# Streamed weights of a recurrent attention and mixer kernel: single blocks instead of pairs, and the mixer's transfers issued from GpSimd

## The chip, the cores and the metric

One core of one Trainium2 chip. The metric is device time of the whole program in microseconds (us); lower is better. A verdict of "faster" or "slower" needs 2%.

## The reference

Four layers one after another on x of 2048 tokens by 640: a recurrent attention with memory (A), a token-shift mixer (B), then A and B again with the same weights. Cut to what matters:

```python
def _A_ref(x, mem0, Wq, Wk, Wv, Wo, seg_len):      # 32 heads of 192, segments of 32 tokens
    mem = mem0                                       # 8 memory tokens
    for s in range(n_seg):                           # 64 segments, strictly in turn
        h = concatenate([mem, x[:, s*32:(s+1)*32]])
        q, k, v = h @ Wq, h @ Wk, h @ Wv             # weights 640 x 6144 each
        o = softmax(mask(q k^T * scale)) v @ Wo      # weights 6144 x 640
        mem = o[:, :8]                               # the next segment needs it
        outs.append(o[:, 8:])

def _B_ref(x, w1, w2, w3, w4):
    h = gelu(layernorm(x) @ w1)                      # 640 x 640
    x1 = x + shift(h) @ w2                           # 640 x 640
    return x1 + gelu(layernorm(x1) @ w3) @ w4        # 640 x 1536, 1536 x 640
```

## The kernel before

Both A layers run at once, the second five segments behind the first, so that a step's weights serve two segments ("lanes"): 64 + 5 = 69 steps, of which the first five and the last five have one lane. The mixer works on chunks of two steps beside the attention (35 chunks). The weights do not fit on chip. Part of them stays, the rest is streamed in every step through a ring of slots that both users share. A plan in Python, with a model of each engine, fixes every engine's instruction order; the chip then follows that order with semaphores.

```python
RING = 8          # slots of two blocks (2 x 768 columns, bf16) for 128 partitions
RING_A = 7        # at most so many for attention's weights
RING_B = 3        # at most so many for the mixer's
DMA_SKEW = 1.6    # the plan's model of a landing
FLIGHT = 5        # SyncE's transfers in flight: number n waits for number n - 5
...
    def block(t, kind, g, c, due):            # attention's weights, 128 rows of Wq, Wk, Wv or Wo
        ...
        a = cut + (c - cut) // 2 * 2          # pairs of blocks
        if (t, kind, g, a) not in streamed:
            b = ring("ra")

            def fn(op):
                return nc.sync.dma_start(out=T(b)[:, 0:2 * n].rearrange("p (c n) -> p c n", c=2), in_=w_src(kind, g, a, a + 2))
            add("SP", 0.45, due, fn, w=(b,), dma=P * 2 * n * 2, queue="wa")
...
    def load_b(c, nm, n, due):                # the mixer's weights, pairs too
        ...
            def fn(op):
                return nc.sync.dma_start(out=T(b)[:, 0:(e - a) * Dm].rearrange("p (c n) -> p c n", n=Dm), in_=src)
            add("SP", 0.45, due, fn, r=rd, w=(b,), dma=P * (e - a) * Dm * 2, queue="wb")
...
    for o in placed:                          # the count of transfers in flight
        ins = o.fn(o)
        if o.dma and o.e == "SP":
            if len(flight) >= FLIGHT:
                tc.add_manual_dep(ins.ins, flight[-FLIGHT].ins.name, ...)
            flight.append(ins)
```

## Time and profile before

| | before |
|---|---|
| median of 4 runs | 3588.28 us (3584.36 to 3591.39) |
| TensorE (PE) busy | 95% of the span |
| the core's DMA engines busy | 94% |
| streamed transfers | 2277 of attention, 630 of the mixer |

How to read the views: PE is TensorE, DVE VectorE, ACT ScalarE, POOL GpSimd, SP SyncE; L536 is line 536 of the kernel, and `a <- b` says that a waited for b. psk, psq and psv are the products with Wk, Wq and Wv, psy that with Wo; psh, hs and y are the mixer's. wst is a slot of the ring, oT the attention's output that psy reads. wbd is a copy of w1, w3 and a part of w2 that the kernel lays out anew in device memory at its start.

The three stages (five steps of one lane, 59 of two, five of one) have to be read apart. Time of PE that is not work I sort by cause as follows, here and after: the distance between the starts of two consecutive matmuls, less the median distance of that shape, goes to what the trace says ended the wait; "fetch" is a wait that no semaphore ended. The sum of the medians is called PE's floor. The prediction shows the views and says what is in them.

### The profile page before, as it was taken

How to read it: one execution, taken by the hardware profiler on the slowest of the kernel's cores; microseconds unless marked ns; L12 is line 12 of the kernel's file. 1: busy time of each engine (PE TensorE's matmuls, PEld its weight loads, DVE VectorE, ACT ScalarE, POOL GpSimd, SP SyncE). 2: the span in 40 equal slices, each digit the busy share in tenths (PEclk: the TensorE clock that was granted, in tenths of full speed). 3: DMA queues.
4: the chain of work that ended last, by engine and by line, in shares of the span. 5: the costliest groups of instructions: out<-in, count | busy, mean ns of one | idle time of the engine just before them, and what ended most of it. 6: DMA issues, size and time to landing. Idle time of an engine off the chain costs nothing.

```text
span 3584.0 us, 188496 instructions
## 1 busy us (share of the span) xinstructions
PE 3387.8 (95%) x84703; PEld 3256.1 (91%) x84703; DVE 2375.3 (66%) x7085; ACT 1709.2 (48%) x3584; POOL 306.2 (9%) x522
## 2 busy tenths in 40 slices
PE   5889999999999999999999999999999999999996
PEld 4778999999999999999999999999999999999875
DVE  2456767767667666776666777776667667776555
ACT  2344545545455544455445554554545445544432
POOL 2000000000000000000000000000000000000000
PEclk9999999999999999999999999999999999999998
DMA  9999999999999999999999999999999999999996
GB/s 341 314 308 306 309 298 309 306 302 315 307 310 323 310 299 304 303 301 312 303 305 310 303 299 303 313 312 300 310 318 309 302 304 306 308 309 310 321 310 212
DMA packets 804793, 1097.18 MB, mean 306 GB/s; under 512 B 51982, under 2 KB 800540, under 8 KB 803984
## 3 DMA queue, kind: packets, MB, share of 16 engines
q1 hardware_dynamic: 795472, 1069.06, 91.2%
q0 software_dynamic: 8512, 16.08, 1.4%
q8 instruction: 662, 10.85, 1.2%
q14 instruction: 147, 1.20, 0.1%
HBM read 1079.68 MB, written 8.19 MB: 304 GB/s over the span
## 4 chain that ended last, share of the span: by engine, by line
PE 86%; DMA 8%; issue 4%; DVE 0%; ACT 0%; POOL 0%; SPq 0%; POOLq 0%; DVEq 0%; ACTq 0%
PE psy L675 16%; PE psk L536 15%; PE psv L577 15%; PE psq L536 15%; PE psvt L589 5%; PE pso L656 4%; PE pss L608 4%; PE psh L999 3%; DMA wst<-in_B_w_dram 3%; PE y L1017 3%; PE pst L641 2%; DMA wst<-in_A_Wk_dram 2%; PE hs L967 1%; DMA wst<-in_A_Wv_dram 1%; PE psh L945 1%
## 5 line engine op out<-in xcount | busy, mean ns | idle before, releaser
L536 PEld LDWEIGHTS <-wst 128*128 128x128 bf16 x13248 | 561.5, 100 | 36.0 <-issue 19.3
L662 DVE CAST oT<-pso 128x480 bf16<-128x480 f32 (+1 forms) x552 | 341.7, 619 | 379.7 <-PE pso L656 377.3
L593 ACT COPY V<-psvt 80x768 bf16<-80x768 bf16 (+1 forms) x552 | 438.4, 794 | 309.0 <-PE psvt L589 302.2
L675 PE MATMUL psy<-oT,wo 128*128 128x80 bf16 (+1 forms) x10350 | 491.6, 199 | 15.3 <-issue 8.6
L577 PE MATMUL psv<-hT,wv 128*128 128x80 bf16 (+1 forms) x9936 | 480.5, 199 | 12.3 <-issue 10.7
L544 ACT CAST qT<-psq 128x480 bf16<-128x480 f32 (+1 forms) x552 | 292.1, 529 | 400.5 <-PE psq L536 398.9
L536 PE MATMUL psq<-hT,wq 128*128 128x80 bf16 (+1 forms) x9936 | 454.2, 199 | 19.6 <-issue 10.0
L583 ACT CAST vTs<-psv 128x480 bf16<-128x480 f32 (+1 forms) x552 | 291.2, 528 | 362.7 <-PE psv L577 359.5
L536 PE MATMUL psk<-hT,wk 128*128 128x80 bf16 (+1 forms) x9936 | 452.8, 199 | 11.7 <-issue 9.3
L619 DVE CUSTOM_DVE_ANT_1 pss<-pss,mask 80x320 f32<-80x320 f32 (+1 forms) x512 | 246.0, 481 | 294.3 <-PE pss L608 287.8
L577 PEld LDWEIGHTS <-wv 128*128 128x128 bf16 x9936 | 408.4, 99 | 30.0 <-issue 11.0
L675 PEld LDWEIGHTS <-wo 128*128 128x128 bf16 x10350 | 413.3, 99 | 23.4 <-issue 15.3
L536 PEld LDWEIGHTS <-wq 128*128 128x128 bf16 x9936 | 395.2, 100 | 31.2 <-issue 13.3
L536 PEld LDWEIGHTS <-wk 128*128 128x128 bf16 x9936 | 397.9, 100 | 25.4 <-issue 14.3
L536 PE MATMUL psk<-hT,wst 128*128 128x80 bf16 (+1 forms) x6624 | 367.9, 199 | 12.1 <-issue 6.5
L577 PE MATMUL psv<-hT,wst 128*128 128x80 bf16 (+1 forms) x6624 | 353.2, 199 | 12.4 <-issue 8.2
L675 PE MATMUL psy<-oT,wst 128*128 128x80 bf16 (+1 forms) x6210 | 335.4, 199 | 11.2 <-issue 10.4
L536 PE MATMUL psq<-hT,wst 128*128 128x80 bf16 (+1 forms) x6624 | 331.6, 199 | 12.4 <-issue 9.4
L626 ACT ACTIVATE pss<-pss,sm 80x320 f32<-80x320 f32 (+1 forms) x552 | 262.0, 475 | 151.5 <-DVE sm L619 151.5
L631 DVE TENSOR_REDUCE sm<-pss 80x4 f32<-80x320 f32 (+1 forms) x552 | 252.3, 457 | 116.4 <-ACT pss L626 115.7
L552 DVE CAST kT<-psk 128x320 bf16<-128x320 f32 (+1 forms) x552 | 254.0, 460 | 112.7 <-PE psk L536 109.3
L646 ACT COPY PT<-pst 80x320 bf16<-80x320 bf16 (+1 forms) x552 | 221.9, 402 | 220.2 <-PE pst L641 218.1
(117 smaller groups left out, 5256.9 us busy)
## 6 DMA issues: line engine op xcount, KB each, us to landing
wst<-in_A_Wk_dram SPq DMA_DIRECT2D x552, 384.0 KB, 5.2
wst<-in_A_Wq_dram SPq DMA_DIRECT2D x552, 384.0 KB, 5.2
wst<-in_A_Wv_dram SPq DMA_DIRECT2D x552, 384.0 KB, 5.2
wst<-in_A_Wo_dram SPq DMA_DIRECT2D x621, 320.0 KB, 5.0
wst<-wbd SPq DMA_DIRECT2D x280, 320.0 KB, 5.1
wst<-in_B_w_dram SPq DMA_DIRECT2D x280, 320.0 KB, 5.7
wst<-wbd SPq DMA_DIRECT2D x70, 160.0 KB, 4.4
wk<-in_A_Wk_dram SPq DMA_DIRECT2D x8, 576.0 KB, 6.8
```

Of the source, the lines that this page charges most:

```text
L536: nc.tensor.matmul(out=o[:, c, 0:N], lhsT=w[:, c * P:(c + 1) * P], rhs=h[:, kc, c0:c0 + N], start=pq.begin(), stop=True, skip_group_check= ...
L544: nc.scalar.copy(out=q[:, :, 0:N], in_=T(pq)[:, :, 0:N])
L552: nc.vector.tensor_copy(out=k4[:, :, 0::3, 0:N], in_=p4[:, :, 0::2, 0:N])
L577: nc.tensor.matmul(out=o[:, c, 0:N], lhsT=w[:, c * P:(c + 1) * P], rhs=h[:, kc, c0:c0 + N], start=pv.begin(), stop=True, skip_group_check= ...
L583: nc.scalar.copy(out=vs[:, :, 0:N], in_=T(pv)[:, :, 0:N])
L593: nc.scalar.copy(out=V_[0:N, :, 0:Dh], in_=T(pt)[0:N].rearrange("n c f -> n (c f)").rearrange("n (i e) -> n i e", i=HG))
L619: nc.vector.tensor_tensor_reduce(out=o, in0=o, in1=maskt.unsqueeze(1).to_broadcast([N, HG, N]), scale=-scale, scalar=3.0e38, op0=ALU.add, ...
L626: nc.scalar.activation(out=o, in_=o, func=ACT.Exp, bias=sm_[0:N, 0:1], scale=-1.0)
L631: nc.vector.reduce_sum(out=sm_[0:N, 4:4 + HG], in_=o, axis=AX.X)
L646: nc.scalar.copy(out=Pt[0:N, :, 0:N], in_=T(pst)[0:N, :, 0:N])
L662: nc.vector.tensor_copy(out=o_[:, :, 0:N], in_=T(pso)[:, :, 0:N])
L675: nc.tensor.matmul(out=T(psy[j])[:, m - m0, c0:c0 + N], lhsT=w[:, m * P:(m + 1) * P], rhs=o_[:, c, 0:N], start=psy[j].begin(), stop=True, ...
```

## The change

The intent: a smaller grain lets a slot be reused as soon as one block is read, and lets a matmul begin as soon as its one block has landed. The doubled number of transfers is shared between two issuing engines. The bytes of the ring and of SyncE's transfers in flight stay.

```diff
-RING = 8
-RING_A = 7
-RING_B = 3
+RING = 16
+RING_A = 14
+RING_B = 6
+B_SP = False
+POOL_US = 0.9
+SP_US = 0.47
-DMA_SKEW = 1.6
-FLIGHT = 5
+DMA_SKEW = 2.0
+FLIGHT = 10
 ...
-        b.make = lambda: wring.tile([P, 2 * GW], bf16, name="wst", tag=f"r{b.slot}")
+        b.make = lambda: wring.tile([P, GW], bf16, name="wst", tag=f"r{b.slot}")
 ...
-                return nc.sync.dma_start(out=T(b)[:, 0:2 * n].rearrange("p (c n) -> p c n", c=2), in_=w_src(kind, g, a, a + 2))
-            add("SP", 0.45, due, fn, w=(b,), dma=P * 2 * n * 2, queue="wa")
+                return nc.sync.dma_start(out=T(b)[:, 0:n], in_=w_src(kind, g, c, c + 1)[:, 0, :])
+            add("SP", SP_US, due, fn, w=(b,), dma=P * n * 2, queue="wa")
 ...
+        def fn(op):
+            return (nc.sync if B_SP else nc.gpsimd).dma_start(out=T(b)[:, 0:Dm], in_=src)
+        add("SP" if B_SP else "POOL", SP_US if B_SP else POOL_US, due, fn, r=rd, w=(b,), dma=P * Dm * 2, queue="wb")
```

The count of transfers in flight looks at SyncE's alone, so the mixer's are no longer in it.

More of the change, by code (lines that the diff above doesn't have):

```diff
@@ L435, in fn @@
                     return nc.sync.dma_start(out=tl[:], in_=w_src(kind, g, 0, cut))
-                add("SP", 0.45, due, fn, w=(b,), dma=P * cut * n * 2, queue="wa")
+                add("SP", SP_US, due, fn, w=(b,), dma=P * cut * n * 2, queue="wa")
                 resident[kind, g] = b, tl
@@ L439, in block @@
             return b, lambda: tl[:, c, :]
-        a = cut + (c - cut) // 2 * 2
-        if (t, kind, g, a) not in streamed:
+        if (t, kind, g, c) not in streamed:
             b = ring("ra")
             def fn(op):
-                return nc.sync.dma_start(out=T(b)[:, 0:2 * n].rearrange("p (c n) -> p c n", c=2), in_=w_src(kind, g, a, a + 2))
-            add("SP", 0.45, due, fn, w=(b,), dma=P * 2 * n * 2, queue="wa")
-            streamed[t, kind, g, a] = b
-        b = streamed[t, kind, g, a]
@@ L449, in block @@
-        return b, lambda: T(b)[:, (c - a) * n:(c - a + 1) * n]
-    mixer = {}
-    def load_b(c, nm, n, due):
-        a = n - n % 2
-        e = min(a + 2, KC if nm in ("w1", "w2") else FC)
-        if (c, nm, a) not in mixer:
-            b = ring("rb")
-            k = {"w1": a, "w3": KC + a, "w2": KC + FC - 4 + a}.get(nm)
-            if nm == "w4":
-                src, rd = w4_v[:, a:e, :], []
-            elif nm == "w2" and a < 4:
-                src, rd = B_w2.rearrange("(g r) d -> r g d", r=QD)[0:P, a:e, :], []
-            else:
-                src = wbd[k:k + e - a].rearrange("b p n -> p b n")
-                rd = [B("wbd", k + i) for i in range(e - a)]
-            def fn(op):
-                return nc.sync.dma_start(out=T(b)[:, 0:(e - a) * Dm].rearrange("p (c n) -> p c n", n=Dm), in_=src)
-            add("SP", 0.45, due, fn, r=rd, w=(b,), dma=P * (e - a) * Dm * 2, queue="wb")
-            mixer[c, nm, a] = b
-        b = mixer[c, nm, a]
-        return b, lambda: T(b)[:, (n - a) * Dm:(n - a + 1) * Dm]
+                return nc.sync.dma_start(out=T(b)[:, 0:n], in_=w_src(kind, g, c, c + 1)[:, 0, :])
@@ new lines, in block @@
+            add("SP", SP_US, due, fn, w=(b,), dma=P * n * 2, queue="wa")
+            streamed[t, kind, g, c] = b
+        b = streamed[t, kind, g, c]
+        return b, lambda: T(b)[:, 0:n]
+    def load_b(c, nm, n, due):
+        b = ring("rb")
+        k = {"w1": n, "w3": KC + n, "w2": KC + FC - 4 + n}.get(nm)
+        if nm == "w4":
+            src, rd = w4_v[:, n, :], []
+        elif nm == "w2" and n < 4:
+            src, rd = B_w2[QD * n:QD * n + P, :], []
+        else:
+            src, rd = wbd[k], [B("wbd", k)]
+        def fn(op):
+            return (nc.sync if B_SP else nc.gpsimd).dma_start(out=T(b)[:, 0:Dm], in_=src)
+        add("SP" if B_SP else "POOL", SP_US if B_SP else POOL_US, due, fn, r=rd, w=(b,), dma=P * Dm * 2, queue="wb")
+        return b, lambda: T(b)[:, 0:Dm]
```

## The prediction

> **What bounds the kernel now.** I read the page first (busy shares, DMA queues), then three windows cut at the places where the work changes, then PE's waits inside the longest window, then a two-microsecond timeline of one such wait, and last the waits of the DMA-issuing queue.
>
> The page, busy shares and DMA queues:
>
> ```profile
> PE 3387.8 (95%) x84703; PEld 3256.1 (91%) x84703; DVE 2375.3 (66%) x7085; ACT 1709.2 (48%) x3584; POOL 306.2 (9%) x522
> ...
> q1 hardware_dynamic: 795472, 1069.06, 91.2%
> q0 software_dynamic: 8512, 16.08, 1.4%
> q8 instruction: 662, 10.85, 1.2%
> ```
>
> Two things are nearly full: TensorE (95%) and the DMA engines (91.2 + 1.4 + 1.2 = 94% with queue 14). Which of them sets the end has to be read by stage. The program runs 69 recurrent steps; in the first five and the last five only one of the two layers is at work, between them both. Cut there (a step begins where psk's 240 matmuls of it begin):
>
> ```profile
> 0.00:298.80 298.80, 232.67 (x6020) 202.25 (x6021) 124.24 (x479) 99.65 (x248) 35.05 (x65) 0.98 0.97 320
> 298.80:3288.90 2990.10, 2907.95 (x72341) 2838.04 (x72339) 2088.53 (x6034) 1497.83 (x3063) 246.00 (x412) 1.00 0.94 307
> 3288.90:3584.00 295.10, 247.21 (x6351) 215.77 (x6347) 162.51 (x574) 111.69 (x273) 25.10 (x45) 0.90 0.87 284
> ```
>
> First column after the window is its length, then PE's busy time; the last two are the DMA share and GB/s. In the first 299 us DMA is at 97% and PE has holes: that stage is bound by bytes (weights that stay are loaded too). The middle 2990 us, 83% of the time, is PE's: 2908 of 2990 us. I took every start-to-start distance of consecutive matmuls from the trace and put the median of its own shape in place of each: 36 ns for 128x80, 25 for 128x40, 56 for 128x128, 136 for 128x320. That sum, PE's floor in its present order, is 3246 us in all and 2868 us in the middle stage. So the middle stage loses only 122 us, 1.77 us a step of 50.7. PE's waits there tell to whom:
>
> ```profile
> PE psy L675 <- issue: 15.5, 25, 1.4
> PE psq L536 <- issue: 13.1, 21, 2.6
> PE psv L577 <- issue: 13.1, 19, 2.2
> PE y L1017 <- DMA wst<-in_B_w_dram: 10.8, 13, 1.7
> PE psk L536 <- issue: 9.2, 18, 1.1
> ...
> PE psk L536 <- DMA wst<-in_A_Wk_dram: 2.0, 6, 0.5
> ```
>
> "issue" means that PE waited for nothing that a semaphore shows. One of them, at close range:
>
> ```profile
> 1504.91 0.34 PE L577 MATMUL psv<-hT,wv 128*128 128x80 bf16 x5
> 1506.63 0.21 PE L577 MATMUL psv<-hT,wv 128*128 128x80 bf16 x1 [1.38 <-issue]
> ```
>
> It stops in the middle of six matmuls on weights that stay in SBUF. I counted the position of each "issue" stop over 0.3 us in PE's instruction order: 155 stops, 132 us, and nearly every one lies at the same place modulo 256 instructions, 1.3 to 1.6 us after a packet of queue 8 ended. They are waits for instructions. Sorted by cause, the middle stage's 122 us are about 93 us of instruction fetch, 21.5 us of weight transfers and 5 us of DVE; the first stage has 32 us of fetch and 33 us of transfers, the last 32 and 3.
>
> **What the Trainium skill says.** "Runtime: NRT & Kernel Launch", section "Instruction fetch mechanics": instructions come in 16 KiB blocks of 256, fetched by the sequencer's own DMA queue while the block before runs, a cost "mostly hidden". The trace agrees on the block (662 packets of 16384 bytes; 169,408 PE instructions / 256 = 662) and not on the hiding. From PE's entry into a block to the start of the next block's packet the mean is 2.17 us, the packet takes 1.02 us (median), and PE goes on 1.43 us after its end: 4.64 us median, 3.4 to 6.0 between the 5th and 95th percentile, against 5.13 us that a block of 128 matmuls lasts. It is barely hidden on average and not hidden in the tail.
>
> "DMA: Bandwidth & Descriptors", section "Queues, rings and completion order": each DMA engine goes round its queue rows packet by packet. So the fetch shares the engines with the weights. Here its wait grows with what is in flight: 0.95 us with one transfer of SyncE out, 1.52 with two, 1.85 with three, 2.30 with four, 2.38 with five; it flattens.
>
> Same page, section "Issuing engines are not separate DMA queues": issuing from several engines saves sequencer time alone, the 16 engines being the same. No run so far shows it for this load.
>
> "SBUF — State Buffer", the box on DVE blocking DMA: descriptors of a transfer issued from GpSimd are written by GpSimd and can be held up by some DVE instructions. Before, GpSimd's own transfers of 80 KB land in 4.4 to 5.1 us (medians), as late as SyncE's of 384 KB (5.2); so I don't see a great hold-up, but a small transfer is no quicker there.
>
> **The change part by part.**
> 1. *Grain.* 2277 transfers of two attention blocks become 4554 of one; 630 of the mixer become 1190 (34 for each of 35 chunks). Bytes and row sizes (1536 and 1280) stay, and PE's instruction count is the same 169,408 in both built programs, so PE's floor of 3246 us stays. A block is usable as soon as it lands and its slot is free as soon as it is read. This goes for the transfer waits: 21.5 us in the middle stage, some of the first stage's 33 (byte-bound, so mostly not). I count half of the first and a seventh of the second: -11 - 5 = -16 us.
> 2. *Completion packets.* 47,048 packets of 4 bytes at 9 ns come from SyncE's 2941 transfers. 5778 - 2941 = 2837 more, one on each engine: 2837 x 9 ns = 26 us more on each engine, 0.7%. In the middle stage hidden under PE; in the first (8%) some 2 us.
> 3. *Issue.* SyncE issues in 0.37 to 0.43 us. It has now 4588 to issue: about 1.9 ms of 3.58, 66 a step at 0.4 = 26 us of 51. Not a bound. GpSimd gets 34 a chunk of 102 us, at 0.55 us as in its rows now (up to 0.9, which the plan assumes): 19 to 31 us, beside its present 9%. Not a bound in sum, but its instructions are in order, and the layer norm's power instruction can stand behind a transfer that waits for a slot. The plan foresees this; I count +3 us.
> 4. *Rows from GpSimd's queue.* Its packets join four rows: 5120 bytes in 237 ns mean, 59 a row, against 61.8 for a 1280-byte row of queue 1. 9520 rows an engine x 2.5 ns = -24 us, which cancels point 2 (-2 us in the byte-bound first stage).
> 5. *What is in flight.* Before, five double transfers at most, the mixer's among them. Now ten singles (the same bytes) of attention, and up to six mixer blocks outside the count. By the table above SyncE's part barely changes the fetch wait. With a GpSimd transfer out at the trigger, the wait was 0.22 us longer on average (110 cases, 2.13 without). The mixer runs 0.33 blocks/us x some 5 us = 1.7 out, so nearly always. Less mixer load on queue 1 takes some 0.1 to 0.2 back. I count +0.05 us on 662 fetches; about a quarter of them stall now, and each lengthens by it: 662 x 0.27 x 0.05 = +9 us.
>
> Sum: -16 + 2 + 3 - 2 + 9 = -4. To this I add a judgement, not a measurement: the plan's constants for latency and issue were set anew with the change, which orders PE by truer landing times: another -6. 3590 - 10 = 3580 us.
>
> **Rivals.**
> *A: fetch gets worse.* More bytes in flight on two rows make each fetch wait 0.25 us longer. For: the mixer leaves the count, GpSimd's packets are 3 to 4 times as long. Against: the table flattens at five. Worth, from the spread of 0.9 us between fetch and block time: mean stall from 0.16 to 0.25 us, x 662 = +60 us: 3640.
> *B: fetch gets better.* Transfers of half the size land earlier, so as many bytes a second need fewer in flight; queue 1 loses the mixer's 18% of bytes. If the wait falls by 0.25 us, stalls fall by a third to a half, -50 us: with the grain's -16 some 3525. Against: freed slots are filled at once, SyncE waits for slots or for landings most of the time, so depth tends to the cap.
> *C: GpSimd's transfers become the wait.* W4's blocks go by every 1.2 us of plan, six slots are 7.2 us, a landing 5 to 6. Its wait is the largest transfer wait now (10.8 us). At +1 us on a third of 35 x 12 blocks: +140 us if nothing hides it; more likely a fifth of that, 3610.
> *D: nothing.* PE's floor and fetch stay, 3575 to 3590.
>
> The queue's own waits speak for B's counter-argument:
>
> ```profile
> SPq L445 <- PE psy L675: 260.6, 279, 2.5
> SPq L445 <- DMA wst<-in_A_Wk_dram: 209.0, 287, 2.8
> SPq L445 <- DMA wst<-in_A_Wq_dram: 179.1, 274, 2.1
> SPq L445 <- PE psv L577: 177.3, 194, 3.5
> ```
>
> It waits for slots that PE holds and for landings in about equal parts.
>
> **Range and chances.** D and the mixed case are likeliest. The change aims at 55 us of transfer waits at most; a gain over 2% (72 us, under 3518) needs fetch to improve as well (B at its fullest): 0.13. A loss over 2% (over 3662) needs A and C together: 0.10. Within: 0.77. Predicted 3580 us, 8 in 10 between 3515 and 3650.
>
> **What would show it.** Right: the middle stage near 2980 us, "y L1017 <- DMA" under 8 us, psk/psq/psv waits on DMA near nil, "issue" waits of PE in the middle stage between 50 and 80 us in sum as now (they are 60 in the view), queue 8 still 662 packets. Wrong: "issue" sums over 100 (A) or under 35 (B); PE waits on wst from wbd or B_w over 30 us, or DVE's vb waiting on GpSimd's st (C). If PE's own floor moves away from 3246 us, the working is wrong at its root.

## The result, and the profile after

The changed kernel takes 3576.96 us (median of 4 runs, 3575.23 to 3581.83) against 3588.28: ratio 0.9971, 95% interval 0.9954 to 0.9988. Ratios here are the mean time of one kernel's runs over that of the other's of the same rounds, so not quite the ratio of the medians. Another chip, five rounds, gave 0.9976 (0.9964 to 0.9989). The gain is small and real.

The page of the changed kernel, busy shares and DMA queues (packets, MB, share of the 16 engines' span):

```profile
PE 3398.9 (95%) x84703; PEld 3260.5 (91%) x84703; DVE 2384.2 (67%) x7085; ACT 1710.5 (48%) x3584; POOL 948.2 (27%) x1712
...
q1 hardware_dynamic: 669504, 874.19, 74.6%
q0 software_dynamic: 65632, 211.12, 17.9%
q8 instruction: 662, 10.85, 1.3%
```

The mixer's 195 MB are now on queue 0: in the trace 152,320 packets of 1280 bytes are gone from queue 1, and 38,080 of 5120 bytes have come to queue 0. The sum of both queues' shares is what it was (92.6 and 92.5%). The middle stage by the same window, and PE's waits in it (us in total, times, longest):

```profile
299.40:3274.80 2975.40, 2910.38 (x72318) 2837.07 (x72318) 2090.98 (x6028) 1498.98 (x3058) 782.56 (x1407) 1.00 0.94 308
```

```profile
PE psk L530 <- DMA wst<-in_A_Wk_dram: 17.3, 31, 1.4
PE y L1011 <- DMA wst<-in_B_w_dram: 13.3, 25, 1.5
PE psq L530 <- DMA wst<-in_A_Wq_dram: 9.6, 14, 1.4
PE psv L571 <- issue: 4.0, 5, 1.0
PE psv L571 <- DMA wst<-in_A_Wv_dram: 2.3, 4, 0.9
...
PE psy L669 <- issue: 1.7, 4, 0.7
```

The stage is 15 us shorter, about the gain. But the list is turned round. Before, "issue" (the wait for instructions) headed it with rows of 15.5, 13.1, 13.1 and 9.2 us and attention's weights came far below; now weights head it and "issue" is nearly gone.

| middle stage, us | before | changed | changed, second profile |
|---|---|---|---|
| length | 2990.1 | 2975.5 | 2961.4 |
| PE's floor | 2867.8 | 2864.3 | 2864.8 |
| waits for instruction fetch | 93.1 | 24.8 | 29.7 |
| waits for weight transfers | 21.5 | 72.0 | 51.0 |
| the rest (DVE, ACT, small ones) | 7.7 | 14.4 | 15.9 |

The second profile is of the other chip; the split of one profile is good to some 20 us, and both say the same. So the change took 68 us away at fetch and gave 50 back at the transfers (63 and 30 in the second). Of the transfers' 50, 45 are attention's: sorted by whose weights PE waited for, attention's waits went from 6 to 51 us and the mixer's from 15 to 21. "Little moved" is the sum of two large moves.

SyncE's queue shows the same from the other side (its waits before are in the prediction):

```profile
SPq L447 <- PE psy L669: 307.5, 472, 2.1
SPq L447 <- PE psk L530: 273.1, 429, 2.4
SPq L447 <- PE psq L530: 222.6, 389, 1.9
SPq L447 <- PE psv L571: 205.0, 378, 3.0
```

Before, waits for landings (the count of five) stood among the longest; now those for slots lead. These sums rank the causes and don't measure idle time: they run into the issuing itself, and the time in which SyncE issues nothing for over 0.15 us fell in the middle stage, from 1913 to 1038 us. So I counted who holds the slots in the middle stage, pairing each transfer with the matmuls that read it, from issue to last read:

| | slots held by the mixer | by attention | held of all |
|---|---|---|---|
| before (8 double slots) | 1.82 | 5.54 | 7.36 of 8 |
| changed (16 single slots) | 5.61 | 9.16 | 14.77 of 16 |

In doubles the mixer went from 1.82 to 2.81 slots, attention from 5.54 to 4.58. GpSimd has its own queue and no count: it asks for the next mixer block whenever one of its six slots is free, however far off its use. The blocks of the first mixer matrix lie landed for some 25 us before they are read. Attention's blocks are in exchange asked for later: from the end of the issue to the first read k's had 7.4 us in the median before and have 5.9 now, against a landing that takes 4.7 and 4.3 us counted from the same moment (the page counts from the issue's start: 5.2 and 4.7). What is left over fell from 2.7 to 1.6 us. GpSimd's blocks of 160 KB land in 4.9 to 5.1 us by the page, SyncE's of the same size (Wo's) in 4.4.

**Theory S** (slots): the new issuer takes slots early; attention's transfers go out later; the DMA queue is shorter, so fetch gets through sooner and weights come later. **Rival G**: the grain alone does it. **Theory B**: bytes set the pace, and PE's stalls are the same waiting under different names; **rival E**: PE sets it.

### The profile page after: what moved, and what is told of

It reads as the page before. It is cut to its first block, busy times and chain, and to the rows that moved or that the text cites. A ratio compares the mean times of both kernels' runs of the same rounds, so it can differ in the third digit from the quotient of the medians.

```text
span 3573.5 us, 194593 instructions
## 1 busy us (share of the span) xinstructions
PE 3398.9 (95%) x84703; PEld 3260.5 (91%) x84703; DVE 2384.2 (67%) x7085; ACT 1710.5 (48%) x3584; POOL 948.2 (27%) x1712
## 4 chain that ended last, share of the span: by engine, by line
PE 69%; DMA 19%; issue 9%; POOL 2%; DVE 1%; ACT 0%; POOLq 0%; SPq 0%; ACTq 0%; DVEq 0%
PE psy L669 14%; PE psq L530 12%; PE psv L571 11%; PE psk L530 11%; DMA wst<-in_A_Wk_dram 7%; DMA wst<-in_A_Wq_dram 5%; PE psvt L583 4%; DMA wst<-in_B_w_dram 4%; PE pss L602 3%; PE pso L650 3%; PE psh L993 3%; DMA wst<-in_A_Wv_dram 3%; PE pst L635 2%; PE y L1011 2%; POOL wst L465 1%
## 5 line engine op out<-in xcount | busy, mean ns | idle before, releaser
L530 PEld LDWEIGHTS <-wst 128*128 128x128 bf16 x13248 | 551.9, 100 | 75.1 <-DMA wst<-in_A_Wk_dram 41.3
L465 POOL DMA_DIRECT2D wst<-in_B_w_dram x560 | 303.6, 542 | 1005.2 <-PE psk L530 250.6
L465 POOL DMA_DIRECT2D wst<-wbd x630 | 339.6, 539 | 724.8 <-PE pss L602 229.5
L669 PE MATMUL psy<-oT,wo 128*128 128x80 bf16 (+1 forms) x10350 | 509.6, 199 | 11.2 <-DMA wo<-in_A_Wo_dram 5.1
L530 PE MATMUL psk<-hT,wk 128*128 128x80 bf16 (+1 forms) x9936 | 482.7, 199 | 7.9 <-ACT hT L707 4.2
L571 PE MATMUL psv<-hT,wv 128*128 128x80 bf16 (+1 forms) x9936 | 466.6, 199 | 6.5 <-DMA wv<-in_A_Wv_dram 4.3
L669 PEld LDWEIGHTS <-wo 128*128 128x128 bf16 x10350 | 425.6, 100 | 21.3 <-issue 9.2
L530 PEld LDWEIGHTS <-wk 128*128 128x128 bf16 x9936 | 411.6, 99 | 21.9 <-issue 8.8
L571 PE MATMUL psv<-hT,wst 128*128 128x80 bf16 (+1 forms) x6624 | 368.0, 199 | 8.7 <-DMA wst<-in_A_Wv_dram 4.8
L669 PE MATMUL psy<-oT,wst 128*128 128x80 bf16 (+1 forms) x6210 | 353.0, 199 | 1.0 <-DMA wst<-in_A_Wo_dram 0.5
```

The lines of the kernel that those rows point to most:

```text
L465: return (nc.sync if B_SP else nc.gpsimd).dma_start(out=T(b)[:, 0:Dm], in_=src)
L530: nc.tensor.matmul(out=o[:, c, 0:N], lhsT=w[:, c * P:(c + 1) * P], rhs=h[:, kc, c0:c0 + N], start=pq.begin(), stop=True, skip_group_check= ...
L571: nc.tensor.matmul(out=o[:, c, 0:N], lhsT=w[:, c * P:(c + 1) * P], rhs=h[:, kc, c0:c0 + N], start=pv.begin(), stop=True, skip_group_check= ...
L669: nc.tensor.matmul(out=T(psy[j])[:, m - m0, c0:c0 + N], lhsT=w[:, m * P:(m + 1) * P], rhs=o_[:, c, 0:N], start=psy[j].begin(), stop=True, ...
```

## The experiments

Each ratio is to the kernel before on the same chip and in the same rounds. The kernel before took 3574.32, 3573.80 and 3569.57 us (medians) in the three batches.

| run | what | ratio (95%) | fetch, us | transfers, us | mixer / attention slots |
|---|---|---|---|---|---|
| before | pairs, SyncE | 1 | 93 | 22 | 1.82 / 5.54 of 8 |
| e3 | pairs, mixer from GpSimd | 1.0133 (1.0114 to 1.0152) | 56 | 62 | 2.92 / 4.74 of 8 |
| e1 | singles, all from SyncE | 1.0269 (1.0245 to 1.0293) | 9 | 153 | 2.76 / 9.31 of 16 |
| changed | singles, mixer from GpSimd | 0.9971 (0.9954 to 0.9988) | 25 | 72 | 5.61 / 9.16 of 16 |

(fetch and transfers: waits of the middle stage.)

### e1: all single blocks from SyncE

```diff
-B_SP = False
+B_SP = True
```

> The changed kernel with the mixer's single blocks issued from SyncE again, inside the count of ten. Theory S (slots): GpSimd takes ring slots for the mixer as soon as they are free (the mixer held 5.6 of 16 slots in the changed kernel, 1.8 of 8 double ones in the kernel before), so attention's weights come later; with SyncE issuing, the mixer's hold falls to 3.5 to 4.5 slots, PE's transfer waits in the middle stage fall from 72 us to 20 to 40, fetch waits rise from 25 us to 60 to 100, time 3575 to 3590. Rival G (grain alone thins the queue, the issuer does not matter): fetch and transfer waits stay at 25 and 72 us.

Measured: 1.0269. PE's waits in the middle stage:

```profile
PE y L1011 <- DMA wst<-in_B_w_dram: 54.8, 62, 2.2
PE psh L993 <- DMA wst<-wbd: 39.0, 28, 3.4
PE psq L530 <- ACT V L587: 21.0, 29, 0.7
PE psv L571 <- DMA wst<-in_A_Wv_dram: 13.9, 18, 1.4
...
PE psq L530 <- issue: 0.9, 2, 0.5
```

Both theories missed. The mixer's hold fell as S said (5.61 to 2.76, even under the 3.5 expected), but attention did not take the slots (9.16 to 9.31): 3.9 of 16 lie empty. SyncE's issuing instructions take 2730 us of the 3675 us span (2055 us in the changed kernel, 1244 before); most take 0.33 to 0.38 us, but 668 of 5778 take over 0.6 us, 1.26 us on average. One in-order queue of 5778 transfers does not refill the slots in time. With so little in flight fetch all but vanishes (9 us), and weights are late (153 us, of which 111 are the mixer's).

### e7: the same with 16 in flight

```diff
-FLIGHT = 10
+FLIGHT = 16
```

> The kernel of the first experiment (all single blocks from SyncE, ratio 1.027 to before) with 16 in flight instead of ten, so that no count binds. Theory I (SyncE's one queue, 5778 issues at 0.33 to 0.38 us and over 1 us in some, can't refill slots in time: 12.1 of 16 slots were held): ratio stays 1.015 to 1.035, held slots stay under 13. Rival C (the count of ten, now shared with the mixer, held it back): ratio falls to 1.00 or lower and held slots rise to 14 or more.

Measured: 1.0273 (1.0242 to 1.0303); 2.77 and 9.35 slots held, 12.1 of 16. Theory I holds: the count is not what binds e1. Whether it is the bare issuing time or the fixed order (one transfer whose slot is still read holds up all behind it) these two runs don't separate; both belong to having one queue for 5778 transfers. The trace of e1 leans to the first: in its middle stage of 3064 us the issues and the 0.1 us between one and the next fill 2683 us, and 380 us are left in longer pauses (1038 of 2975 in the changed kernel).

### e3: the issuer alone

```diff
-                return nc.sync.dma_start(out=T(b)[:, 0:(e - a) * Dm]...
-            add("SP", 0.45, due, fn, r=rd, ...
+                return nc.gpsimd.dma_start(out=T(b)[:, 0:(e - a) * Dm]...
+            add("POOL", 0.9, due, fn, r=rd, ...
```

> The kernel before (double blocks, 8 slots, five in flight) with one thing changed: the mixer's double transfers issued from GpSimd, outside the count. It tells the issuer from the grain. Theory S (GpSimd fetches the mixer as early as slots allow, attention gets fewer slots, less is in flight): the mixer's hold rises from 1.8 to over 2.5 of 8 slots, fetch waits of the middle stage fall from 93 us to under 50, transfer waits rise from 21 us to over 60; time within 1% of before. Rival G (the single grain thins the queue): fetch waits stay over 75 us and transfer waits under 35.

Measured: 1.0133 (median 3618.16 us; the profiled run, with a span of 3602.0 us, is among its quick ones). PE's waits in its middle stage:

```profile
PE psk L536 <- DMA wst<-in_A_Wk_dram: 19.8, 32, 1.6
PE psv L577 <- DMA wst<-in_A_Wv_dram: 8.0, 18, 1.2
PE psk L536 <- issue: 7.5, 16, 0.7
PE psv L577 <- issue: 7.1, 8, 2.2
...
PE y L1017 <- DMA wst<-in_B_w_dram: 3.2, 5, 1.1
```

S holds in kind: the mixer's hold went from 1.82 to 2.92 slots, attention's fell from 5.54 to 4.74, its weights became the longest waits, and the mixer's own wait (10.8 us before) shrank. In size it is near: transfers 62 us as expected, fetch 56 and not under 50. The time is over the 1% that I allowed, and the stalls of this profile don't account for it: they grew by 11 us in the middle stage, where the median grew by 44. G is refuted for the transfers' part: without any change of grain they trebled (attention's from 6 to 51 us, as in the changed kernel). The grain is still needed for the rest of fetch's fall, 56 to 25.

So each half of the change costs by itself, 1.3% and 2.7%, and together they gain 0.3%. The single grain needs a second issuer; the second issuer costs attention slots. That the single grain makes up for it, as a slot is held shorter, fits the traces (k's from issue to last read, means: 8.0 us before, 7.2 in e3, 6.7 in the changed kernel), but no run shows it by itself.

### e2: the mixer held to four slots

```diff
-RING_B = 6
+RING_B = 4
```

> The changed kernel with the mixer held to 4 of the 16 slots instead of 6, still from GpSimd. Theory S: attention gets 12 slots, its transfer waits fall from some 45 us to under 25 in the middle stage, more is in flight and fetch waits rise from 25 to 40 to 70 us; the sum of both stays near 97 us within 25, time within 0.7% of the changed kernel. Mixer waits (y on B_w) may grow. Rival P (GpSimd's transfers are themselves slow): attention's waits do not fall, mixer's waits rise above 40 us, time over 3600.

Measured: 1.0050 (1.0027 to 1.0073), 0.8% over the changed kernel's 0.9971. Slots as meant: mixer 3.69, attention 11.16. In the middle stage attention's waits fell from 51 to 6 us, as S says, but the mixer's rose from 21 to 53 (over the whole span y 23.5 us and psh 12.5), and psy waited 23.7 us for DVE's oT (1.9 in the changed kernel), as the plan orders PE's work differently. Fetch stayed at 24 us; I had expected 40 to 70. More slots for attention do not of themselves put more in flight: landings took 4.2 us instead of 4.3 at the same rate.

### e4: six in flight

```diff
-FLIGHT = 10
+FLIGHT = 6
```

> The changed kernel with six of SyncE's single transfers in flight instead of ten. Theory F (what is in flight sets the fetch wait, a mean of 1.82 us from trigger to packet in the changed kernel): at a cap of six, which binds half the time (five to seven are out on average), the fetch wait falls to 1.3 to 1.6 us and fetch stalls of the middle stage from 25 to under 15 us, while transfer waits rise from 72 to 90 to 140: time 0.3 to 2% over the changed kernel. If fetch does not depend on what is in flight: fetch wait and stalls as they were.

Measured: 1.0433 (1.0411 to 1.0455). The fetch part came out: trigger to packet 1.47 us, fetch 10 us. The time did not: 4.6% over the changed kernel, not 0.3 to 2. Transfer waits fell to 54 us instead of rising, but the plan knows of the cap, takes the weights to be later still and orders PE's work around it. These are the longest waits of PE over the whole span:

```profile
PE psk L530 <- ACT hT L707: 44.0, 29, 1.9
PE psy L669 <- DVE oT L656: 40.7, 119, 0.5
PE psk L530 <- DMA wst<-in_A_Wk_dram: 21.2, 31, 1.8
```

PE stands between its own steps instead of at the weights. The run shows that fetch depends on what is in flight, and nothing clean of what a cap costs.

**Fetch and what is in flight.** Rate times mean time from issue to landing gives the bytes in flight (worked out from each trace, us 300 to 3200), beside the mean time from PE's entry into a block of 256 instructions to the start of the next block's packet:

| run | in flight, MB | trigger to packet, us |
|---|---|---|
| e6 (below) | 1.10 | 1.41 |
| e1 | 1.17 | 1.41 |
| e4 | 1.22 | 1.47 |
| e2 | 1.31 | 1.75 |
| e8 (below) | 1.34 | 1.76 |
| changed | 1.35 | 1.82 |
| e5 (below) | 1.43 | 1.84 |
| before | 1.44 | 2.17 |
| e3 | 1.48 | 2.05 |

Over nine kernels it rises with the bytes in flight, and in e4 a smaller cap lowered both (with the order of work that the plan made for it). The bytes are not all of it: at the same 1.43 to 1.44 MB e5 (single blocks) waits 1.84 us and the kernel before (pairs) 2.17, and e3 waits less than before with more in flight. The same shows inside the traces: with 0.9 to 1.2 MB of weights out at the entry the mean is 1.96 us before, 1.69 in e3, 1.56 in the changed kernel; with 1.5 to 1.8 MB they agree (2.30, 2.26, 2.25). What makes up the rest, the grain or the second queue, these runs don't separate. Fetch stalls follow, though e3, with 2.05 us, stalls 56 us against 93 for 2.17: time that PE spends waiting for weights also gives the fetch time to catch up.

### e5 and e6: does PE or do the bytes set the pace?

e5 leaves matmuls out (wrong result), e6 transfers (wrong result):

```diff
-                        for c in range(GC):
+                        for c in range(GC if kc < KC - 1 else 1):
```

```diff
+        n -= n % 2
+        if (c, nm, n) in mixer:
+            b = mixer[c, nm, n]
+            return b, lambda: T(b)[:, 0:Dm]
-        b = ring("rb")
+        b = mixer[c, nm, n] = ring("rb")
```

> The changed kernel with 5 of 6 matmuls left out in the last of five contractions of k and q, wrong result on purpose; order, transfers and bytes as they were. It takes 80 matmuls of 36 ns from a step, 2.88 us of PE: 59 x 2.88 = 170 us in the middle stage. Theory B (bytes set the pace, the stalls are only PE waiting for them in one form or another): the middle stage shortens by less than 60 us, DMA rate stays below 315 GB/s there, stalls grow from 111 us to over 210. Rival E (PE sets the pace, stalls are latency): it shortens by 130 to 200 us, DMA rate rises to 320 GB/s or more.

> The changed kernel with every second mixer block not loaded (the block before it is used twice, wrong result on purpose): 560 of 5744 streamed transfers and 91.8 of 1098 MB (8.4%) fewer, PE's work as it was. Theory B: the stalls of the middle stage (111 us) fall to under 40 us, time 3480 to 3510. Rival E: stalls fall in part, by a quarter to a half, time 3515 to 3555, as latency under a less full queue gets only somewhat shorter.

The middle stages of e5 and e6:

```profile
291.60:3181.60 2890.00, 2773.13 (x67599) 2681.19 (x67599) 2083.67 (x6029) 1503.11 (x3059) 784.64 (x1407) 1.00 0.96 317
292.80:3209.60 2916.80, 2894.97 (x72319) 2832.84 (x72319) 2073.72 (x6031) 1512.03 (x3060) 533.38 (x941) 1.00 0.90 288
```

Measured: e5 0.9744 (0.9718 to 0.9770, "faster"), e6 0.9782 (0.9760 to 0.9803, "unclear" at 2%). Against the changed kernel (0.9971) that is 2.3% and 1.9%, some 81 and 68 us. e5's middle stage is 2890 us, 85 shorter for 170 us of matmuls taken out; DMA moves 317.5 GB/s and stalls rise from 111 to 195 us. In e6 the stalls fall from 111 to 52 us (fetch 25 to 10, transfers 72 to 29), for 8.4% fewer bytes. The stages lie between the two theories (e6's time alone, 3495 us, is in B's range): half of the matmul time taken away shows, and half of the stalls go with the bytes. Neither side is the bound alone; with 94% of the DMA engines' time used and 96% of the middle stage PE's floor, each saving on one side is partly eaten by the other.

### e8 and e10: a better version?

The first mixer matrix asked for only after its chunk's layer norm:

```diff
+        power = plan.ops[-1]
 ...
-                wb, wv = load_b(c, "w1", n, due)
+                wb, wv = load_b(c, "w1", n, due, (power,))
```

> The changed kernel with the first mixer matrix's five blocks asked for only after the layer norm's power instruction of their chunk. In the changed kernel they lay landed for 25 us before use and held 1.5 of 16 slots for it. Theory S: the mixer's hold falls from 5.6 to 4.2 to 5 slots, attention's rises from 9.2 to about 10, attention's transfer waits in the middle stage fall from 47 us to 25 to 40; time 0.2 to 0.8% under the changed kernel, if no new wait on the first matrix comes (its lead falls to 8 to 12 us against a landing of 5). Rival: the freed slots are taken by the second matrix of the mixer; no change in attention's waits, time within 0.2%.

Measured: 0.9982 (0.9967 to 0.9998). Slots: mixer 3.72, attention 10.9. Transfer waits fell from 72 to 41 us (attention's from 51 to 11, the mixer's up from 21 to 29) and fetch from 25 to 18, but DVE waits rose from 10 to 38, again psy for oT. The theory's step holds, the gain of 0.2 to 0.8% does not come. To compare on one chip, it was run again beside the changed kernel:

> The changed kernel as it is, five rounds, so that the next runs can be compared with it on one chip. Ratio to before 0.995 to 1.000, as on record (0.9971). Middle stage: fetch waits near 25 us, transfer waits near 72.

> The kernel with the first mixer matrix asked for later, again, beside the changed kernel on the same chip. Theory S, after its first run (fetch 18, transfers 41, but DVE waits 38 instead of 10): ratio to before 0.994 to 1.000, the changed kernel's within 0.3% of it, as what is won at the transfers is half lost where psy waits for oT. If it is truly better: 0.5% under the changed kernel or more.

Measured: changed 0.9976 (0.9964 to 0.9989), this one 0.9991 (0.9978 to 1.0004). It is no better. Is its DVE wait due to the plan's late landing times?

> The kernel with the first mixer matrix later, and the plan's landing time back at 1.6 us. If PE's order for late transfers is what brings its DVE waits (38 us in the middle stage against 10), they fall under 15 us and the ratio to before is 0.985 to 0.994. If not, they stay over 25 us and the ratio is that of the kernel beside it within 0.3%.

Measured with the landing time back at 1.6 us: 1.0052 (1.0035 to 1.0068). The DVE waits did fall, from 38 to 9 us, and transfer waits rose from 43 to 83. So the question's answer is yes, and the ratio that I had expected (0.985 to 0.994) was wrong: the order that waits less for DVE waits more for weights.

### e11: the two constants alone

```diff
-DMA_SKEW = 1.6
+DMA_SKEW = 2.0
 ...
-add("SP", 0.45, ...
+add("SP", 0.47, ...
```

> The kernel before with only the plan's two constants of the changed one (landing time 2.0 us added instead of 1.6; 0.47 us an issue instead of 0.45). The prediction put -6 us (-0.17%) on this as a judgement. Right: ratio 0.996 to 1.000 and transfer waits of the middle stage under 21 us. Rival: the constants do nothing of themselves, or cost as the order of PE's work is made for transfers later than they are: 1.000 to 1.010.

Measured: 0.9986 (0.9964 to 1.0008): not told apart from nothing. Transfer waits of the middle stage 14 us instead of 21.5, fetch 86 instead of 93. The size fits what I had judged; it is not shown.

No run beat the changed kernel.

## Why the prediction was right

The time, 3577 us for a predicted 3580, and "same" are right. The working was not: two steps failed by more than their size and nearly cancelled. That the sum came within 3 us is luck; what was sound is PE's floor, which leaves little to win or lose. Of the signs that the prediction named, the stage's length (2975 us) and queue 8 came out right; y's wait, attention's waits "near nil" and the "issue" sum did not (11 us in the view, under the 35 that it gave as the sign of rival B).

1. *Grain, -16 us.* Wrong in sign. Transfer waits of the middle stage rose by 50 us (30 in the second profile), and y's wait on the mixer's weights rose from 10.8 to 13.3 us instead of falling under 8. I took the lead of a transfer as given and counted only what the grain adds to it. What sets the lead is how many slots each stream gets (e3: the issuer alone brings the sum to 62 us, and e2 and e8, which give slots back, take attention's from 51 to 6 and 11), and how fast one queue can refill them (e1: the grain alone brings it to 153 us).
2. *Completion packets, +2 us.* As said: 2837 more on each engine at 9 ns. No wait of PE shows them.
3. *Issue, +3 us.* Right for the changed kernel: SyncE issues for 2055 us, 58%, a little over the 1.9 ms I worked out, since 518 issues take over 0.6 us, 1.13 us on average; GpSimd's take 0.54 us and it is busy 27%. DVE's longest wait on GpSimd's power instruction (vb for st) is 13.2 us in sum over the whole span, 9.4 before: near the +3 us that I counted, though a wait of DVE is not yet time of the kernel. What I did not see is that issuing is why the mixer had to leave SyncE at all: e1.
4. *Rows from GpSimd's queue, -2 us.* A joined packet of 5120 bytes took 243 ns on average, 61 a row, against 62.8 for a 1280-byte row of queue 1 in the same trace: a small saving of the sign I said, and the busy share stayed 94%.
5. *What is in flight, +9 us.* The largest miss: fetch fell by 68 us. The step took SyncE's ten places to be as full as the five before, and set more transfers on queue 0 on top. In fact SyncE had 3.9 pairs out on average before and 5.6 singles now (rate of issues times mean time to landing), with 1.5 blocks of the mixer beside them, so the depth fell in sum, from 1.44 to 1.35 MB. That is a part of fetch's fall; the other part stays open, as e5 has 1.43 MB and waits no longer for it. This is rival B of the prediction without its gain in time. B's counter-argument ("freed slots are filled at once") was true, but the filler was the mixer, whose blocks then lie landed and are not in flight. That SyncE waits for slots and for landings "in about equal parts" was a loose reading too: over the whole view it is 1499 us to 1024.
6. *Constants, -6 us.* e11 gives 0.14% less, not clear of nothing.

Rival A (fetch worse) did not come, nor did C: the mixer's waits stayed under its sign of 30 us (21 in the middle stage). That attention's weights would be the ones to come late, no rival named. PE's floor was 3246 us before and 3243 after, as the prediction rests on.

Of the swap, the transfers' half (slots and issuer) is shown by e3 one way and by e2 and e8 the other, and e1 and e7 show why the mixer could not stay on SyncE. Fetch's half is shown in part: e4's cap moves it together with the bytes in flight, the rest is not separated, and the kernels' orders of work differ too. Not settled: what makes some of SyncE's issues take 1.1 to 1.3 us.

## What to carry to other kernels

When a change moves the time little, sort the stalls by cause before believing that nothing happened: here 68 us went and 50 came. Two streams that share one ring of buffers are tied by who asks first, so moving one of them to another issuer, with its own queue and no count, changes the other's lead. Halving the transfers' size doubles the issuing, and on one queue that cost 2.7% before it gained anything.

## What the Trainium skill lacked or had wrong

- "Runtime: NRT & Kernel Launch", section "Instruction fetch mechanics", calls the cost of crossing an instruction block mostly hidden. By the sum that holds here: 93 us of waits for some 565 blocks of the middle stage before, 0.16 us each. But they were three quarters of PE's stalls there, and the section doesn't say that a weight stream beside it lengthens the fetch: the waits were 25 us in the changed kernel and 9 in e1, with less in flight. PE's fetch has one block's time (5.1 us) and took 4.6 us in the median before, 4.3 after.
- "DMA: Bandwidth & Descriptors", section "Issuing engines are not separate DMA queues", says that issuing from several engines saves only sequencer time, usually small relative to the DMA itself. For one transfer that holds here (0.47 us in e1, against a landing of 4.3 to 4.5), in sum it doesn't: with 5778 transfers of 160 to 192 KB on SyncE alone that time was 2730 of 3675 us and 3.9 of 16 buffers lay empty: 1.0269, against 0.9971 with 1190 of them moved to GpSimd. How much of the loss is issuing time and how much the fixed order of one queue is not separated.
- Missing on the pages that I read, a measured figure for what joined rows bring on this chip: GpSimd's transfers of 1280-byte rows went in packets of 5120 bytes, four rows in 196 ns (median), where SyncE's went row by row in 55 ns each.
- Missing too: that some of SyncE's issues take far longer than the rest: 11% of them in the changed kernel took over 0.6 us (1.13 us on average), 8% before (0.96 us), where most took 0.33 to 0.38 us.
